# Two weight folds placed together, with one weight load moved forward and two weight loads cut into smaller pieces

## The chip, the cores and the metric

The kernel runs on one core of a Trainium2 chip. The core has five engines that run their own instruction streams: TensorE (PE in the profile, with its weight loads listed as PEld), VectorE (DVE), ScalarE (ACT), GpSimd (POOL) and SyncE (SP). Here SyncE issues all DMA transfers. The metric is the time of one execution on the device in microseconds; the median over the runs counts.

## The reference

One token sequence of 2048 rows and 512 columns in bfloat16 goes through a layer norm, then through a linear attention and, in parallel, a gated feed-forward part; both are added to the input.

```python
xn = _layernorm(x)
# attention, 32 heads of width 16
qkv = (xn @ wqkv)                       # 512 -> 3 * 512, by heads
pq, pk = q @ w_phi[h], k @ w_phi[h]     # 16 x 16 per head
phi = concat(softmax(p), softmax(-p))   # for q and for k
kv, z = phi_k^T v, sum over s of phi_k
o = (phi_q kv) / (phi_q z + 1e-6)
# feed-forward, width 1792
h = (xn @ w_gate) * (xn @ w_up)
out = x + o @ wo + h @ w_down
```

## The kernel before

The 2048 tokens are 16 tiles of 128 (n = 0 to 15), four tiles to a group (T = 0 to 3). The normalized tokens are kept transposed in xnT (features on the partitions). Tiles 0 to 3 are transposed on TensorE. For the others, `ln_block` leaves a list of chores: statistics on VectorE, the inverse deviation on GpSimd, the normalized tile `xn` on ScalarE and a DMA transpose into xnT issued by SyncE (L222). `chore(k)` runs the next k of them.

The feature weights are folded once: wq and wk are each multiplied by the block-diagonal of w_phi, so that W1q and W1k give pq and pk straight from xnT. `fold` does half of one of them: it needs `wT2`, which holds wq and wk transposed by a DMA from device memory (index 0 is wq, 1 is wk), and `bd`, the block-diagonal. It fills two PSUM banks with 16 small matmuls of 64 rows (two row halves side by side) and copies one bank on ScalarE and one on VectorE. `fold_both` calls it for both halves. The W1k fold stands between units 2 and 3; the W1q fold stands at tile 7 of the main loop, and the load of wq's transposed part is issued at L450, just before that loop.

A unit (T, f) of the feed-forward part is four matmuls for the gate block f, four for the up block f (each 128x512, over one group of tokens), a ScalarE copy of the gate and a VectorE product into hT. There are 14 blocks (FC) for each of 4 groups. `ffn(k)` issues the next k units. The units fill the time of TensorE between the projections: `vkproj(n)` computes v and the k features of tile n (eight matmuls), `features` makes exponentials on ScalarE, sums and reciprocals on VectorE and the product on GpSimd, `kv(n)` adds the tile to the attention state, and `qproj(n)` makes the q features. Later `attend` and `fin` finish each tile.

The order on every engine is written out by hand: the program's order is the order of each engine's stream. SyncE's stream begins with the loads at L84 to L102: x tiles 0 to 3 between pieces of wv, gate and up weights of blocks 0 to 3, w_phi, wk transposed (L96), gate and up blocks 4 to 8 (L97), x tiles 4 to 7 (L98), blocks 9 to 13 (L99), x tiles 8 to 15, w_down, wo. The transposes of xnT tiles 4 to 7 come behind them in the same queue.

Eight PSUM banks are there. Six of them rotate (`bank`, pool ps_s) for all projections, units and folds; the other two belong in turn to pv of tiles 0 and 1 (pool ps_v), to the attention state (ps_k) and to the attention output (ps_ab).

Of the kernel before, what the change touches and what calls it, by code (L numbers as in the profile page):

```python
# [16 lines left out]
def _bcast_ap(ap_in: bass.AP, new_ap):  # L17
    return bass.AP(tensor=ap_in.tensor, offset=ap_in.offset, ap=new_ap)
# [3 lines left out]
def kernel(  # L22
# [12 lines left out]
    nc = tc.nc  # L35
    P = 128
    S, D = A_x.shape[-2], A_x.shape[-1]
# [4 lines left out]
    DC = D // P  # L42
    FC = F // P
# [3 lines left out]
    TT = GT * P  # L47
# [16 lines left out]
    wv = wpool.tile([P, DC, D], BF16)  # L64
# [7 lines left out]
    wT2 = hpool.tile([P, 2, DC, D], BF16, name="wT2", tag="h")  # L72

    def dma_x(lo, hi):
        nc.sync.dma_start(out=xall[:, lo:hi, :], in_=x_view(lo, hi))  # L75

    def dma_cols(eng, w, src, lo, hi, at=0):
        eng.dma_start(out=w[:, :, lo - at:hi - at], in_=src[:, lo:hi].rearrange("(c p) f -> p c f", p=P))

    def dma_gu(lo, hi):  # L80
        dma_cols(nc.sync, wg, B_w_gate, lo * P, hi * P)
        dma_cols(nc.sync, wu, B_w_up, lo * P, hi * P)
# [3 lines left out]
    for lo in (0, 2):  # L86
        nc.sync.dma_start(out=wv[:, lo:lo + 2, :],  # L87
                          in_=A_wqkv[lo * P:(lo + 2) * P, 2 * D:3 * D].rearrange("(c p) f -> p c f", p=P))
# [4 lines left out]
    dma_cols(nc.sync, wu, B_w_up, 0, 2 * P)  # L93
    nc.sync.dma_start(out=wphi[:], in_=A_w_phi.rearrange("(c h) d f -> (h d) c f", c=DC))
    dma_gu(2, 4)
    nc.sync.dma_start(out=wT2[:, 1, :, :], in_=A_wqkv[:, D:2 * D], transpose=True)  # L96
    dma_gu(4, 9)  # L97
    dma_x(4, 8)  # L98
    dma_gu(9, FC)  # L99
    dma_x(8, NT)  # L100
    nc.sync.dma_start(out=wd[:], in_=B_w_down.rearrange("(c p) d -> p c d", p=P))
    nc.sync.dma_start(out=wo[:], in_=A_wo.rearrange("(c p) n -> p c n", p=P))  # L102
# [25 lines left out]
    W1q = wpool.tile([P, DC, D], BF16)  # L128
    W1k = wpool.tile([P, DC, D], BF16)
# [20 lines left out]
    def bank(name, dt=F32, n=TT):  # L150
        return ps_s.tile([P, n], dt, name=name, tag="s")
# [49 lines left out]
    def chore(k=1):  # L201
        for _ in range(min(k, len(chores))):
            chores.pop(0)()
# [40 lines left out]
        nc.vector.tensor_tensor(out=bd[:], in0=_bcast_ap(bo, [bo.ap[0], [0, DC], [E1, 8], [1, DH]]),  # L244
                                in1=_bcast_ap(wp, [wp.ap[0], [DH, DC], [0, 8], [1, DH]]), op=ALU.mult)

    def fold(qk, dst, j0):
        R = P // 2
        banks = [bank("pq").rearrange("p (j c x) -> p j c x", j=2, c=DC) for r in range(2)]
        for j in range(2):  # L250
            for c in range(DC):
                for r in range(2):
                    rows = slice(r * R, (r + 1) * R)
                    nc.tensor.matmul(banks[r][:, j, c, :], lhsT=wT2[rows, qk, c, (j0 + j) * P:(j0 + j + 1) * P],  # L254
                                     rhs=bd[rows, c, 4 * r:4 * r + 4, :].rearrange("p a b -> p (a b)"),
                                     start=True, stop=True)
        dv = dst[:, j0:j0 + 2, :].rearrange("p j (c r x) -> p r j c x", c=DC, r=2)
        nc.scalar.copy(out=dv[:, 0], in_=banks[0])
        nc.vector.tensor_copy(out=dv[:, 1], in_=banks[1])

    def fold_both(qk, dst):
        for j0 in (0, 2):
            fold(qk, dst, j0)

    def proj(ps, n, w, js=range(DC)):
        for j in js:
            nc.tensor.matmul(ps, lhsT=xnT[:, j, n * P:(n + 1) * P], rhs=w[:, j, :],  # L267
                             start=(j == 0), stop=(j == DC - 1))
# [21 lines left out]
    def qproj(n):  # L290
        phiq = features(n, W1q, "q")
        phiqTs[n] = qtpool.tile([P, NG, P], BF16, name="phiqT")
        nc.sync.dma_start(out=phiqTs[n][:], in_=phiq[:].rearrange("p g c -> p (g c)"), transpose=True)

    hTs = {}
    units = [(T, f) for T in range(NGRP) for f in range(FC)]

    def half(w, name, T, f, lo, hi):
        ps = bank(name)[:, 0:hi - lo]
        for c in range(DC):  # L300
            nc.tensor.matmul(ps, lhsT=w[:, c, f * P:(f + 1) * P], rhs=xnT[:, c, T * TT + lo:T * TT + hi],  # L301
                             start=(c == 0), stop=(c == DC - 1))
        return ps

    def gate_copy(ps, n):
        g_sb = gpool.tile([P, TT], BF16, name="g_sb")
        nc.scalar.copy(out=g_sb[:, 0:n], in_=ps)  # L307
        return g_sb

    def hidden(T, f, ps, g_sb, lo, hi):  # L310
        if T not in hTs:
            hTs[T] = hpool.tile([P, FC, TT], BF16, name="hT", tag="h")
        nc.vector.tensor_tensor(out=hTs[T][:, f, lo:hi], in0=ps, in1=g_sb[:, 0:hi - lo], op=ALU.mult)  # L313

    def unit(T, f, lo=0, hi=TT):
        pg = half(wg, "g", T, f, lo, hi)
        pu = half(wu, "u", T, f, lo, hi)
        hidden(T, f, pu, gate_copy(pg, hi - lo), lo, hi)

    def ffn(k):  # L320
        for _ in range(k):
            if units:
                unit(*units.pop(0))
# [31 lines left out]
    def vcopy(n, ps, eng=nc.scalar):  # L355
        dst, src = vts[n % NV][:, :, :, 0:DH], ps.rearrange("p (a b c) -> p a b c", a=8, b=4)
        if n >= GT:
            nc.scalar.copy(out=dst, in_=src)  # L358
        elif eng is nc.scalar:
            nc.scalar.activation(out=dst, in_=src, func=AF.Identity, scale=rst[:, n:n + 1])  # L360
        else:
            eng.tensor_scalar(out=dst, in0=src, scalar1=rst[:, n:n + 1], scalar2=None, op0=ALU.mult)

    with tc.tile_pool(name="ps_v", bufs=1, space=PSUM) as ps_v:
        pv = [ps_v.tile([P, D], F32, name=f"pv{n}") for n in range(2)]
# [32 lines left out]
        nc.gpsimd.tensor_tensor(out=r2[:], in0=rst[:], in1=rst[:], op=ALU.mult)  # L398
        nc.gpsimd.tensor_tensor(out=M4[:], in0=BO[:, 0:4, :], in1=BO[:, 4:8, :], op=ALU.add)

    with tc.tile_pool(name="ps_k", bufs=1, space=PSUM) as ps_k:
        kvps = [ps_k.tile([P, 4, 4, E1], F32, name=f"kv{b}") for b in range(2)]
        phiks = {}

        def kproj(n, pf=None):
            phiks[n] = features(n, W1k, "k", pf)

        def vkproj(n, apart=False):
            pv, pk = bank("pv"), bank("k")
            for js in (range(DC),) if apart else [(j,) for j in range(DC)]:  # L410
                proj(pv, n, wv, js)
                proj(pk, n, W1k, js)
            vcopy(n, pv)
            kproj(n, pk)

        def kv(n):
            vt, phik = vts[n % NV], phiks[n]
            for gr in range(NG):
                nc.tensor.matmul(kvps[gr // 4][:, gr % 4, :, :].rearrange("p a b -> p (a b)"),  # L419
                                 lhsT=phik[:, gr, :], rhs=vt[:, gr, :, :].rearrange("p a b -> p (a b)"),  # L420
                                 start=(n == 0 and gr % 4 == 0), stop=(n == NT - 1 and gr % 4 == 3))

        for f in range(2):
            unit(0, f, 2 * P, TT)
        del units[0:2]
        ffn(1)
        fold_both(1, W1k)
        ffn(1)
        ln_block(4)
        ffn(1)  # L430
        chore(2)
        kproj(0)
        ffn(1)
        chore(2)
        ffn(1)
        chore()
        kproj(1)
        ffn(1)
        chore()
        ffn(1)  # L440
        kproj(2)
        chore()
        ffn(1)
        kv(0)
        chore()
        kproj(3)
        chore()
        ffn(1)
        kv(1)
        nc.sync.dma_start(out=wT2[:, 0, :, :], in_=A_wqkv[:, 0:D], transpose=True)  # L450
        for n in range(GT, NT):
            if n in (4, 8):
                ln_block(n + 4)
            if n == 7:
                fold_both(0, W1q)
            vkproj(n, apart=n == 7)
            chore(1 if n % GT < 2 else 0)
            ffn(1)
            kv(n - 2)
            if n == 6:  # L460
                ffn(1)
            chore((1, 2, 2, 2)[n % GT])
            if n >= 8 and n % 2 == 0:
                qproj((n - 8) // 2)
            if n != 6:
                ffn(1)
        ffn(1)
        kv(NT - 2)
        ffn(1)
        kv(NT - 1)  # L470
        for b in range(2):
            nc.vector.tensor_tensor(out=KV[:, 4 * b:4 * b + 4, :, :], in0=kvps[b][:],
                                    in1=_bcast_ap(M4[:], [M4[:].ap[0], [0, 4], [E1, 4], [1, E1]]), op=ALU.mult)
        qproj(4)
        ffn(1)
# [65 lines left out]
```

## Time and profile before

| what | value |
|---|---|
| median of 3 runs | 221.17 us (221.03 to 221.37) |
| profiled execution | 221.16 us |
| its span | 219.5 us |
| TensorE clock granted | 1.00 |
| VectorE busy | 140.0 us |
| ScalarE busy | 88.4 us |
| GpSimd busy | 72.8 us |
| read from device memory | 8.67 MB |

Busy times are sums over the span; an engine can be busy much of it without setting the end. A row of the costliest groups gives line, engine, operation, what it writes and reads, the count, the busy time and the mean of one. Times "to landing" of a DMA count from the start of its issue on SyncE until its completion is signalled.

### The profile page before, as it was taken

To read this page: it belongs to the slowest core of one execution; us is meant where nothing else is said; L and a number is where in the kernel's file an instruction comes from. 1 tells how busy PE (TensorE), PEld (TensorE's weight loads), DVE (VectorE), ACT (ScalarE), POOL (GpSimd) and SP (SyncE) were. 2 spreads that over 40 slices of the span, in tenths; PEclk is the share of its full clock that TensorE was granted. 3 is DMA by queue.
4 is the path that set the end of the run, shared out by engine and by line. 5 is a ranking of instruction groups with operands and counts; after the bars stand their busy time and mean duration, and the time that the engine had idled before them with its cause. 6 is when DMAs were issued, how large, how long until landed. Compare 5 with 4: busy or idle time off the path is not lost.

```text
span 219.5 us, 3521 instructions
## 1 busy us (share of the span) xinstructions
PE 215.4 (98%) x1307; PEld 104.4 (48%) x1307; DVE 140.0 (64%) x240; ACT 88.4 (40%) x164; POOL 72.8 (33%) x64
## 2 busy tenths in 40 slices
PE   8999999999999999999999999999999999999994
PEld 3564445445444444444544444444444444454443
DVE  5757976887598757667499773196655645454321
ACT  4635496449664775465435212141231322100000
POOL 3600655363348463635145333033023033000000
PEclk9999999999999999999999999999999999999999
DMA  5999994303202241202047345114431431412501
GB/s 156 260 302 390 371 249 99 49 0 51 48 0 48 51 73 24 48 3 48 1 27 121 72 106 118 43 24 96 96 75 24 96 75 25 96 48 72 74 25 48
DMA packets 47249, 19.91 MB, mean 91 GB/s; under 512 B 37504, under 2 KB 46976, under 8 KB 47104
## 3 DMA queue, kind: packets, MB, share of 16 engines
q1 hardware_dynamic: 47232, 19.69, 38.7%
q8 instruction: 10, 0.16, 0.3%
q14 instruction: 7, 0.06, 0.1%
HBM read 8.67 MB, written 2.10 MB: 49 GB/s over the span
## 4 chain that ended last, share of the span: by engine, by line
PE 96%; DMA 2%; SPq 1%; issue 0%; DVE 0%
PE g L301 22%; PE fin L331 22%; PE u L301 22%; PE fin L334 6%; PE k L267 6%; PE q L267 6%; PE pv L267 6%; DMA wv<-in_A_wqkv_dram 2%; PE kv L419 2%; PE ab L483 2%; SPq L75 1%; PE pq L254 1%; SPq L87 0%; DVE o_sb L342 0%; PE tp L235 0%
## 5 line engine op out<-in xcount | busy, mean ns | idle before, releaser
L301 PE MATMUL u<-xnT,wu 128*128 128x512 bf16 (+1 forms) x232 | 57.8, 372 | 0.0
L301 PE MATMUL g<-xnT,wg 128*128 128x512 bf16 (+1 forms) x232 | 57.7, 372 | 0.0
L307 ACT CAST g_sb<-g 128x512 bf16<-128x512 f32 (+1 forms) x58 | 33.4, 576 | 48.6 <-PE g L301 48.4
L313 DVE TENSOR_TENSOR hT<-u,g_sb 128x512 bf16<-128x512 f32 (+1 forms) x58 | 37.1, 648 | 24.6 <-PE u L301 15.5
L286 POOL TENSOR_TENSOR phiq<-e,rs 128x1024 bf16<-128x1024 f32 x16 | 30.9, 1932 | 62.9 <-DVE rs L284 54.1
L282 DVE TENSOR_REDUCE sums<-e 128x64 f32<-128x1024 f32 x32 | 38.9, 1216 | 20.2 <-ACT e L278 20.2
L331 PE MATMUL fin<-wd,hT 128*128 128x512 bf16 (+2 forms) x238 | 51.1, 366 | 0.0
L286 POOL TENSOR_TENSOR phik<-e,rs 128x1024 bf16<-128x1024 f32 x16 | 30.9, 1931 | 43.9 <-DVE rs L284 30.3
L301 PEld LDWEIGHTS <-wu 128*128 128x128 bf16 x232 | 22.7, 98 | 25.6
L331 PEld LDWEIGHTS <-hT 128*128 128x128 bf16 x238 | 22.4, 98 | 24.8
L301 PEld LDWEIGHTS <-wg 128*128 128x128 bf16 x232 | 22.0, 98 | 23.6
L267 PEld LDWEIGHTS <-xnT 128*128 128x128 bf16 x192 | 17.3, 98 | 18.8 <-ACT xnT L238 1.3
L267 PE MATMUL pv<-wv,xnT 128*128 128x512 bf16 x64 | 22.1, 381 | 0.4 <-DMA wv<-in_A_wqkv_dram 0.2
L267 PE MATMUL k<-W1k,xnT 128*128 128x512 bf16 x64 | 21.8, 379 | 0.0
L342 DVE TENSOR_TENSOR o_sb<-fin,xall 128x512 bf16<-128x512 f32 (+2 forms) x13 | 8.5, 651 | 20.5 <-PE fin L334 20.5
L284 DVE RECIPROCAL rs<-sums 128x64 f32<-128x64 f32 x32 | 17.7, 553 | 3.1
L334 PE MATMUL fin<-wo,oT 128*128 128x512 bf16 (+2 forms) x68 | 16.6, 366 | 0.0
L267 PE MATMUL q<-W1q,xnT 128*128 128x512 bf16 x64 | 16.4, 378 | 0.0
L276 ACT ACTIVATE e<-q 128x512 f32<-128x512 f32 x12 | 7.2, 597 | 22.2 <-PE q L267 22.2
L358 ACT CAST vt<-pv 128x512 bf16<-128x512 f32 x12 | 7.1, 588 | 16.4 <-PE pv L267 16.4
L493 DVE TENSOR_TENSOR otok<-ab,rden 128x512 bf16<-128x512 f32 x16 | 11.1, 691 | 0.6
L157 DVE BATCH_NORM_STATS2 stats<-xall 128x6 f32<-128x512 bf16 x16 | 10.7, 670 | 1.0 <-DMA xall<-in_A_x_dram 1.0
(60 smaller groups left out, 126.3 us busy)
## 6 DMA issues: line engine op xcount, KB each, us to landing
out_dram<-o_sb SPq DMA_DIRECT2D x15, 128.0 KB, 1.9
wd<-in_B_w_down_dram SPq DMA_DIRECT2D x1, 1792.0 KB, 15.4
wg<-in_B_w_gate_dram SPq DMA_DIRECT2D x2, 640.0 KB, 6.9
wu<-in_B_w_up_dram SPq DMA_DIRECT2D x2, 640.0 KB, 8.0
xall<-in_A_x_dram SPq DMA_DIRECT2D x1, 1024.0 KB, 11.7
xall<-in_A_x_dram SPq DMA_DIRECT2D x4, 128.0 KB, 2.5
wv<-in_A_wqkv_dram SPq DMA_DIRECT2D x2, 256.0 KB, 3.6
wg<-in_B_w_gate_dram SPq DMA_DIRECT2D x2, 256.0 KB, 4.8
```

Of the source, the lines that this page charges most:

```text
L157: nc.vector.bn_stats(out=stats[:], in_=xall[:, n, :])
L267: nc.tensor.matmul(ps, lhsT=xnT[:, j, n * P:(n + 1) * P], rhs=w[:, j, :], start=(j == 0), stop=(j == DC - 1))
L282: nc.vector.tensor_reduce(out=sums[:], in_=ev, axis=AX.X, op=ALU.add)
L284: nc.vector.reciprocal(out=rs[:].rearrange("p a b -> p (a b)"), in_=sums[:])
L286: nc.gpsimd.tensor_tensor(out=phi[:].rearrange("p g (x f) -> p (g x) f", f=DH), in0=ev, in1=rs[:].to_broadcast((P, 2 * H, DH)), op=ALU.mult)
L301: nc.tensor.matmul(ps, lhsT=w[:, c, f * P:(f + 1) * P], rhs=xnT[:, c, T * TT + lo:T * TT + hi], start=(c == 0), stop=(c == DC - 1))
L307: nc.scalar.copy(out=g_sb[:, 0:n], in_=ps)
L313: nc.vector.tensor_tensor(out=hTs[T][:, f, lo:hi], in0=ps, in1=g_sb[:, 0:hi - lo], op=ALU.mult)
L331: nc.tensor.matmul(ps, lhsT=hTs[T][:, f, t4 * P:(t4 + 1) * P], rhs=wd[:, f, lo:lo + w], start=(f == 0), stop=False)
L334: nc.tensor.matmul(ps, lhsT=oTs[n][:, c, :], rhs=wo[:, c, lo:lo + w], start=False, stop=(c == DC - 1))
L342: nc.vector.tensor_tensor(out=o_sb[:], in0=ps, in1=xres, op=ALU.add)
L493: nc.vector.tensor_tensor(out=o_tok[:].rearrange("p (b h d) -> p b h d", b=2, d=DH), in0=abv[:, :, :, 0:DH], in1=rden[:].to_broadcast((P, ...
```

## The change

Four things change. The load of wq's transposed part moves from L450 to right behind wk's. Gate and up weights of blocks 4 to 13 come in loads of blocks 4 and 5, 6 to 9 and 10 to 13, with x tiles 4 to 7 behind the first of them. The second halves of units 0 and 1, then units 2 and 3, then all four half folds follow each other; the first half of W1q uses the two banks that held pv of tiles 0 and 1, so the folds stand now within that pool's scope. In the main loop the W1q fold, the special place of one unit at tile 6, and the form of `vkproj` that does v's four matmuls before k's at tile 7 are gone.

```diff
-    nc.sync.dma_start(out=wT2[:, 1, :, :], in_=A_wqkv[:, D:2 * D], transpose=True)
-    dma_gu(4, 9)
+    for qk in (1, 0):
+        nc.sync.dma_start(out=wT2[:, qk, :, :], in_=A_wqkv[:, qk * D:(qk + 1) * D], transpose=True)
+    dma_gu(4, 6)
     dma_x(4, 8)
-    dma_gu(9, FC)
+    dma_gu(6, 10)
+    dma_gu(10, FC)
     dma_x(8, NT)
...
-    def fold(qk, dst, j0):
+    def fold(qk, dst, j0, pq):
         R = P // 2
-        banks = [bank("pq").rearrange("p (j c x) -> p j c x", j=2, c=DC) for r in range(2)]
+        banks = [ps.rearrange("p (j c x) -> p j c x", j=2, c=DC) for ps in pq]
...
-    def fold_both(qk, dst):
-        for j0 in (0, 2):
-            fold(qk, dst, j0)
...
         nc.gpsimd.tensor_tensor(out=M4[:], in0=BO[:, 0:4, :], in1=BO[:, 4:8, :], op=ALU.add)
 
+        for f in range(2):
+            unit(0, f, 2 * P, TT)
+        del units[0:2]
+        ffn(2)
+        for qk, dst in ((1, W1k), (0, W1q)):
+            for j0 in (0, 2):
+                own = qk == 0 and j0 == 0
+                fold(qk, dst, j0, [ps[:] if own else bank("pq") for ps in pv])
+
...
-        def vkproj(n, apart=False):
-            pv, pk = bank("pv"), bank("k")
-            for js in (range(DC),) if apart else [(j,) for j in range(DC)]:
-                proj(pv, n, wv, js)
-                proj(pk, n, W1k, js)
-            vcopy(n, pv)
+        def vkproj(n):
+            ps, pk = bank("pv"), bank("k")
+            for j in range(DC):
+                proj(ps, n, wv, (j,))
+                proj(pk, n, W1k, (j,))
+            vcopy(n, ps)
             kproj(n, pk)
...
-        for f in range(2):
-            unit(0, f, 2 * P, TT)
-        del units[0:2]
-        ffn(1)
-        fold_both(1, W1k)
-        ffn(1)
         ln_block(4)
         ffn(1)
...
-        nc.sync.dma_start(out=wT2[:, 0, :, :], in_=A_wqkv[:, 0:D], transpose=True)
         for n in range(GT, NT):
             if n in (4, 8):
                 ln_block(n + 4)
-            if n == 7:
-                fold_both(0, W1q)
-            vkproj(n, apart=n == 7)
+            vkproj(n)
             chore(1 if n % GT < 2 else 0)
             ffn(1)
             kv(n - 2)
-            if n == 6:
-                ffn(1)
             chore((1, 2, 2, 2)[n % GT])
             if n >= 8 and n % 2 == 0:
                 qproj((n - 8) // 2)
-            if n != 6:
-                ffn(1)
+            ffn(1)
```

## The prediction

> **What bounds the kernel now.** I read the page's first and fourth parts first, then TensorE's own timeline, then SyncE's, and last the load of the DMA engines by stretches.
>
> ```profile
> PE 215.4 (98%) x1307; PEld 104.4 (48%) x1307; DVE 140.0 (64%) x240; ACT 88.4 (40%) x164; POOL 72.8 (33%) x64
> PE 96%; DMA 2%; SPq 1%; issue 0%; DVE 0%
> ```
>
> TensorE is busy 98% of the span, and the chain that ended last is TensorE's for 96%. In the list of waits of that engine only two stand, 0.8 us at the start and 0.2 us before the first projections. So from about 7 us on the time is the sum of TensorE's instructions in their order. An edit can gain only by taking work off TensorE, and it loses whatever stall it puts there.
>
> What the two folds cost on TensorE is read from the chain in order of time (start us, us, what):
>
> ```profile
> 15.38 0.57 PE pq L254 x32
> 15.96 0.97 PE g L301 x4
> 16.93 0.86 PE u L301 x4
> ...
> 50.14 0.57 PE pq L254 x32
> 50.72 0.97 PE pv L267 x4
> 51.69 0.86 PE k L267 x4
> ```
>
> A fold of both j halves is 32 small matmuls in 0.57 us, and the four full matmuls right behind it take 0.97 where others of their size take 0.86: each return from 64-row to 128-row tiles costs 0.11 us.
>
> The loads all go through SyncE's queue (start us, us of issue):
>
> ```profile
> 7.28 3.53 SPq L96 DMA_TRANSPOSE wT<-in_A_wqkv_dram  x1
> 10.86 0.58 SPq L78 DMA_DIRECT2D wg<-in_B_w_gate_dram  x1
> ...
> 16.10 8.28 SPq L102 DMA_DIRECT2D wo<-in_A_wo_dram  x1
> 28.69 7.08 SPq L222 DMA_TRANSPOSE xnT<-xn  x4
> 35.82 2.16 SPq L450 DMA_TRANSPOSE wT<-in_A_wqkv_dram  x1
> ```
>
> The load of wq's part stands behind all others at 35.82, after the four transposes of token tiles 4 to 7. How full the DMA engines are comes from the stretches (columns: stretch, its us, then busy us and count for PE, PEld, DVE, ACT, POOL, then TensorE's clock, DMA share, GB/s):
>
> ```profile
> 11.00:12.00 1.00, 1.00 (x7) 0.52 (x6) 0.38 (x1) 0.09 (x1) 0.00 (x0) 1.00 1.28 290
> 12.00:13.00 1.00, 1.00 (x12) 0.90 (x10) 0.98 (x2) 0.37 (x1) 0.00 (x0) 1.00 0.88 117
> 14.00:16.00 2.00, 2.00 (x40) 1.05 (x39) 0.70 (x2) 0.83 (x2) 0.00 (x0) 1.00 1.06 385
> 24.00:30.00 6.00, 6.00 (x30) 2.69 (x28) 5.21 (x10) 3.89 (x7) 5.20 (x6) 1.00 1.08 351
> 30.00:33.00 3.00, 3.00 (x23) 1.47 (x22) 2.32 (x3) 3.00 (x6) 0.85 (x2) 1.00 1.00 157
> ```
>
> Until about 30 us the DMA engines have no free time. And this is where the queue touches TensorE: the transposes of tiles 4 and 5, in the issues of the stretches around 28.7 and 31.0 us:
>
> ```profile
> xnT<-xn SPq DMA_TRANSPOSE x1, 4.3
> ...
> xnT<-xn SPq DMA_TRANSPOSE x1, 2.4
> ```
>
> Tile 4's transpose is issued at 28.69 and lands 4.3 us later, at 33.0; tile 5's needs 2.4 us. The difference is the backlog: wo's load, issued at 16.10 and 16.4 us on its way, lands at 32.5, just ahead of it. TensorE's timeline starts the first projection of tile 4 at 33.68. The slack is 0.7 us.
>
> The page "DMA: Bandwidth & Descriptors" of the Trainium skill (section Queues, rings and completion order) says that each DMA engine takes SyncE's descriptors in ring order; the trace agrees, 4.3 us against 2.4.
>
> **The change part by part.**
>
> *TensorE's work.* The same instructions in another order. The q fold's 0.57 us leaves 50.14 and goes to about 17.1 (units 2 and 3 first, then k's fold, then q's). One of the two returns to full tiles goes: -0.11 us. Interleaving pv and k for tile 7, as for the other tiles, changes no count: in the chain a group of eight such matmuls takes 1.72 us in either form, less the 0.11 after the fold. So TensorE reaches tile 4's projection at 33.68 + 0.57 = 34.25, and without a stall the end moves by -0.11.
>
> *PSUM banks and evictions around the folds.* Unit 3's up matmuls end at 15.38 + 1.73 = 17.11 in the new order. Banks rotate by six; q's first half has the two pv banks, so the only tight pair is q's second half, which takes unit 3's banks. Their reader on VectorE (0.69 us, begun 0.11 us after unit 2's up matmuls in the old trace) is done at 17.91, while three of four halves (48 matmuls of 18 ns) occupy TensorE to 17.97. I price this at 0, bounds 0 to 0.2. Unit 4's gate, at 18.25, needs the first ScalarE copy (0.59 us, from about 17.5): covered. Four copies each on ScalarE (1.07 us a pair) and VectorE (1.28 a pair) run to 19.6 and 20.5, so unit 4's product starts near 20.5 instead of 19.62. Behind it stand tile 4's and 5's statistics and tile 0's k sums; this delays tile 4's normalized tile and the issue of its transpose from 28.69 to some 29.5. With 2.4 us to land that would be 31.9, still ahead of 34.25. So 0 on the path. At 50.9 to 52 four copies go from ScalarE and VectorE; TensorE did not wait there, so nothing is gained.
>
> *The load of wq's part, moved in front.* It passes, on SyncE, ten loads in the new cut (six of gate and up weights, two of x, wd, wo) and four token transposes. The DMA engines are full, so everything behind it shifts by its own time. k's part, the same 512 KB, ran at 290 GB/s in the stretch 11 to 12: 0.524 MB / 290 GB/s = 1.81 us. Lower bound: the stretch 12 to 13, just behind k's transpose, moved 117 GB/s where 385 would go, 0.70 us lost; if the second transpose fills that hole, 1.1. Upper bound: SyncE spent 3.53 us on issuing k's and issues nothing else meanwhile, 3.5. I take 1.81, as the stretch is the same operation under the same load.
>
> The same page (section Latency and other measured facts) gives 261 GB/s for a DMA transpose with a non-contiguous middle dimension; by that it would be 2.0 us and the end 0.2 later. The row decides for 290.
>
> *Gate and up weights in pieces of 2, 4 and 4 column blocks instead of 5 and 5.* Same 2560 KB, 1.28 KB rows cut to 0.5 and 1 KB. Before: 2.62 MB at 377 GB/s (385 in 14 to 16, 369 in 18 to 21) = 6.95 us. After: 0.52 MB at the 301 GB/s of 6 to 9 us, when pieces of 0.5 KB ran, = 1.74, and 2.10 MB at the 351 GB/s of 24 to 30, where wd's and wo's 1 KB rows run, = 5.97. Together 7.71: +0.76 us for all that follows. Bounds 0 (the 301 is mixed with tiny packets of wphi, and rows may cost nothing) to 0.8.
>
> *Sum.* The queue ahead of tile 4's transpose ends 1.81 + 0.76 = 2.57 us later, so the transpose lands at 33.0 + 2.57 = 35.57. TensorE is there at 34.25 and waits 1.32 us; no other matmul can pass. Behind the waiting projection stand, in order, unit 11, kv of tile 2 and all the rest; nothing later has idle time on TensorE to give it back. Total 1.32 - 0.11 = +1.2 us. Against the profiled execution's 221.16 us (span 219.5), which is the median of 221.17 to 0.01: 222.4 us, or 0.5% slower. In general the end moves by the queue's shift less 1.36, and by -0.11 at the least.
>
> **The rivals.**
>
> *The queue is shifted by less than tile 4's slack of 1.25 us* (the other sign: not slower). Place: the landing of tile 4's transpose. Price: none, only the merged fold's -0.11 us remains, 221.05 us; it decides below a shift of 1.25. For it: the 0.70 us hole at 12 to 13 us, and pieces that may cost less than I take: 1.1 + 0 is enough. Against it: DMA share at or above 1 in all stretches but that one, and wo's landing half a microsecond ahead of the transpose's.
>
> *The weights become late first.* The up weights for unit 6 lie now in the load of blocks 6 to 9. Of the old load of blocks 9 to 13 the up part landed at 13.28 + 10.0 = 23.3. Now a wq part (1.81), 0.5 MB in small pieces (1.74) and 1 MB in 1 KB rows (1.05 MB / 351 = 2.99) take the place of 6.95 us: 22.9. Unit 6's up matmuls come at 22.80 + 0.57 = 23.37: in time by 0.5. If the issue time of 3.53 holds, it is 24.6 and TensorE waits 1.2 us there, and the rest of the late transpose's delay falls at tile 4: the landing shifts by 3.53 + 0.76 = 4.29, the end by 4.29 - 1.36 = 2.9, 224.1 us. For it: k's own issue. Against it: that issue came while other loads filled the queue, and the late one took 2.16.
>
> *The merged folds gain more than the one return.* At most all that the q fold costs, 0.57 + 0.11 = 0.68 us: 220.5. For it: nothing but that the small matmuls overlap in two row groups; against it, both folds took the same 0.57 in the old trace, wherever they stood. The change does what it says on SyncE and TensorE, where both orders are written out by hand, so that it does nothing is no case.
>
> **How the numbers follow.** What can be told from no change here is 0.2%, 0.44 us. The forecast (tile 4 waits, shift of 1.8 to 3.3 us) gets 0.54; the shift that stays in the slack, or over it by less than 0.44 + 0.11 us, gets 0.28; the large shift with late weights 0.10; the gain beyond one return 0.08. So faster 0.08, same 0.28, slower 0.64. The forecast's own range is 221.6 to 223.1. The range for 8 in 10 reaches down to the rival without a stall with some spread of single runs (220.9) and up to a shift of 3.9 us (223.7).
>
> **What would show it.** In the changed profile: two fold groups as one run of 64 small matmuls of 1.14 us near 17.1, with one 0.97 behind them; the late fold at 50 gone; a wait of TensorE, or of its weight load, on a DMA at the first projection of tile 4, at 34.3 to 35.6 us; tile 4's transpose landing some 6 us after its issue; wo landing near 35 instead of 32.5. I am wrong if TensorE shows no wait between 30 and 40 us, if wo lands before 33.8, if the wait stands already at units 4 to 6, or if the time is under 221 with the folds shorter than 1.1 us.

## The result and the profile after

The changed kernel takes 223.73 us, the median of 6 runs (223.07 to 226.15), against 221.12 us before (220.98 to 221.37). The ratio of all runs is 1.0145, interval 1.011 to 1.018. Two of the six runs, 225.98 and 226.15 us, had a mean granted clock of 0.992 and the others 0.999 or 1.000; the median of these four is 223.58 us. Forecast were 222.4 us and a range of 220.9 to 223.7: the direction and the place of the wait hold, the size is too small by half. The profiled execution took 223.65 us, its span 221.9 (before 221.16 and 219.5): +2.5 us.

The first and fourth parts of the page of the changed kernel:

```profile
PE 215.4 (97%) x1307; PEld 104.3 (47%) x1307; DVE 140.0 (63%) x240; ACT 88.5 (40%) x164; POOL 72.9 (33%) x64
PE 90%; DMA 3%; DVE 3%; ACT 1%; issue 1%; POOL 1%; DVEq 0%
```

TensorE's busy time is the same to 0.1 us, as it must be when only the order changes. The 2.5 us are idle time of TensorE, and the chain that ended last now runs through a DMA. Who waited for whom, for TensorE and for its weight loads (us in total, times, longest):

```profile
PE pv L265 <- DMA xnT<-xn: 1.8, 1, 1.8
...
PE g L299 <- ACT W1q L260: 0.7, 1, 0.7
...
PEld L299 <- DMA wg<-in_B_w_gate_dram: 0.8, 1, 0.8
```

Two waits have come, and TensorE's timeline shows where (start us, us; in brackets the idle time before):

```profile
16.75 0.64 PE L256 MATMUL pq<-bd,wT 64*128 64x64 bf16 x32
17.22 0.40 PE L256 MATMUL pv<-bd,wT 64*128 64x64 bf16 x16
17.45 0.60 PE L256 MATMUL pq<-bd,wT 64*128 64x64 bf16 x16
18.74 1.04 PE L299 MATMUL g<-xnT,wg 128*128 128x512 bf16 x4 [0.69 <-ACT W1q L260]
...
34.55 0.42 PE L426 MATMUL kv<-vt,phik 128*128 128x68 bf16 x8
36.77 0.39 PE L265 MATMUL pv<-wv,xnT 128*128 128x512 bf16 x1 [1.81 <-DMA xnT<-xn]
```

The second is the forecast one: the first projection of tile 4 starts at 36.77 instead of 33.68, 1.81 us after TensorE was ready. The first, 0.69 us at unit 4, stands against a ScalarE copy in one list and against the gate weights' DMA in the other; the experiments decide for the DMA. It costs nothing here, since tile 4 could not have started earlier anyway: the end moves by 36.77 - 33.68 less the 0.66 us that the late q fold took between its neighbours before, 2.43 us, and the span by 2.4.

SyncE's queue (start us, us of issue), then the landing of wo's load and of tile 4's transpose:

```profile
7.25 5.65 SPq L97 DMA_TRANSPOSE wT<-in_A_wqkv_dram  x2
12.94 0.58 SPq L78 DMA_DIRECT2D wg<-in_B_w_gate_dram  x1
...
14.67 2.64 SPq L78 DMA_DIRECT2D wg<-in_B_w_gate_dram  x1
17.36 0.51 SPq L78 DMA_DIRECT2D wu<-in_B_w_up_dram  x1
```

```profile
wo<-in_A_wo_dram SPq DMA_DIRECT2D x1, 512.0 KB, 14.9
...
xnT<-xn SPq DMA_TRANSPOSE x1, 6.9
```

wo is issued at 21.36 and lands at 36.2 (before 32.5); tile 4's transpose is issued at 29.81 and lands at 36.7 (before 33.0). Both are 3.7 us later. The issue of the gate weights of blocks 6 to 9 took 2.64 us where its neighbours take 0.5. Three stretches of the changed kernel (columns as in the prediction; the last three are TensorE's clock, DMA share, GB/s):

```profile
12.00:13.00 1.00, 1.00 (x12) 0.90 (x10) 1.00 (x3) 0.41 (x2) 0.00 (x0) 1.00 0.74 147
...
17.80:19.00 1.20, 0.51 (x17) 0.28 (x13) 1.20 (x3) 1.20 (x3) 0.00 (x0) 1.00 0.73 150
19.00:22.00 3.00, 3.00 (x16) 1.35 (x15) 2.25 (x4) 1.28 (x3) 0.00 (x0) 1.00 1.07 368
```

The reader is to see two holes: one between the two transposes at 12 to 13 us, and one at 17.8 to 19.0, behind the long issue, where the DMA engines moved 150 GB/s.

### The profile page after: what moved, and what is told of

It reads as the page before. It is cut to its first block, busy times and chain, and to the rows that moved or that the text cites. A ratio compares the mean times of both kernels' runs of the same rounds, so it can differ in the third digit from the quotient of the medians.

```text
span 221.9 us, 3521 instructions
## 1 busy us (share of the span) xinstructions
PE 215.4 (97%) x1307; PEld 104.3 (47%) x1307; DVE 140.0 (63%) x240; ACT 88.5 (40%) x164; POOL 72.9 (33%) x64
## 4 chain that ended last, share of the span: by engine, by line
PE 90%; DMA 3%; DVE 3%; ACT 1%; issue 1%; POOL 1%; DVEq 0%
PE fin L329 22%; PE g L299 20%; PE u L299 19%; PE pv L265 6%; PE fin L332 6%; PE q L265 6%; PE k L265 5%; DMA xnT<-xn 3%; PE ab L478 2%; PE kv L426 2%; PE warm L348 1%; DVE stats L159 1%; DVE hT L311 1%; DVE sums L280 1%; PE tp L237 0%
## 5 line engine op out<-in xcount | busy, mean ns | idle before, releaser
L284 POOL TENSOR_TENSOR phik<-e,rs 128x1024 bf16<-128x1024 f32 x16 | 30.9, 1932 | 46.4 <-DVE rs L282 33.5
L329 PEld LDWEIGHTS <-hT 128*128 128x128 bf16 x238 | 22.4, 98 | 24.8
L265 PEld LDWEIGHTS <-xnT 128*128 128x128 bf16 x192 | 17.3, 97 | 20.7 <-DMA xnT<-xn 1.9
L265 PE MATMUL k<-W1k,xnT 128*128 128x512 bf16 x64 | 22.3, 379 | 0.0
```

The costliest lines, as they stand in the source:

```text
L284: nc.gpsimd.tensor_tensor(out=phi[:].rearrange("p g (x f) -> p (g x) f", f=DH), in0=ev, in1=rs[:].to_broadcast((P, 2 * H, DH)), op=ALU.mult)
L329: nc.tensor.matmul(ps, lhsT=hTs[T][:, f, t4 * P:(t4 + 1) * P], rhs=wd[:, f, lo:lo + w], start=(f == 0), stop=False)
```

## The experiments

The theory: what is queued ahead of tile 4's transpose is pushed back, and TensorE waits there. Rivals: the four half folds in a row cost by their eight copies and banks; the smaller pieces cost by SyncE's issues; tile 4 is late because its normalized tile is late. All times are medians; "lands" is tile 4's transpose in the profiled run.

| kernel | us | ratio to before (interval) | lands | waits of TensorE after 8 us |
|---|---|---|---|---|
| before | 221.1 to 221.2 | | 33.0 | none |
| changed | 223.73 | 1.0145 (1.011 to 1.018) | 36.7 | 0.69 unit 4, 1.81 tile 4 |
| e1 wq's load early, alone | 226.12 | 1.0222 (1.0178 to 1.0266) | 36.1 | 2.3 and 0.7 unit 4 |
| e2 pieces alone | 221.35 | 1.0015 (1.0003 to 1.0027) | 33.6 | none |
| e3 changed, old pieces | 223.68 | 1.0114 (1.0097 to 1.0131) | 36.3 | 1.8 and 0.7 unit 4 |
| e4 changed, wd and wo late | 221.49 | 1.0018 (1.0008 to 1.0028) | 32.0 | 0.3 unit 4 |
| e5 as e4, wq behind blocks 4 and 5 | 222.57 | 1.0083 (1.005 to 1.0115) | 35.9 | 1.7 q fold |
| e6 folds alone | 221.04 | 0.9992 (0.9983 to 1.0001) | 33.8 | none listed |
| e7 changed, wo late | 222.01 | 1.0035 (1.0023 to 1.0047) | 35.1 | 0.6 unit 4 |
| e8 as e4, more warm-up matmuls | 221.96 | 1.0038 (1.0021 to 1.0055) | 31.9 | none |
| e9 as e5, folds behind unit 4 | 221.36 | 1.001 (1.0001 to 1.0019) | 33.8 | 0.3 unit 6 |

### e1, wq's load early, alone

```diff
     nc.sync.dma_start(out=wT2[:, 1, :, :], in_=A_wqkv[:, D:2 * D], transpose=True)
+    nc.sync.dma_start(out=wT2[:, 0, :, :], in_=A_wqkv[:, 0:D], transpose=True)
...
-        nc.sync.dma_start(out=wT2[:, 0, :, :], in_=A_wqkv[:, 0:D], transpose=True)
```

> The kernel before with one edit: the load of wq's transposed part stands right behind wk's; folds and weight pieces stay as they were. Queue theory: all loads behind it shift by 1.8 us (524 KB at 290 GB/s) to 2.5 us (with a stretch in which the DMA engines starve, as in the changed kernel at 17.8 to 19.0 us), tile 4's transpose lands at 34.8 to 35.5 instead of 33.0, TensorE is there at 33.68 and waits 1.1 to 1.8 us: 222.3 to 223.0 us. Theory that the order of the folds makes the loss: no change, 221.1 us.

Measured 226.12 us, far over both. TensorE's waits in e1, and the stretch behind them:

```profile
PE g L302 <- DMA wg<-in_B_w_gate_dram: 2.3, 1, 2.3
...
PE u L302 <- DMA wu<-in_B_w_up_dram: 0.7, 1, 0.7
```

```profile
22.00:27.00 5.00, 5.00 (x18) 2.04 (x17) 2.81 (x6) 1.74 (x3) 0.00 (x0) 0.72 1.05 396
```

With the old large pieces the weights of unit 4 come with 640 KB each and land at 19.9 and 21.6 us, so TensorE stands at unit 4 and not at tile 4; and after 3.0 us of waits the mean granted clock of the next five microseconds was 0.72, an estimated 1.4 us more. The queue itself answers the question: wo, issued at 19.87, takes 15.7 us and lands at 35.6 instead of 32.5. The load moved alone shifts the queue by 3.1 us, not by 1.8.

### e2, the pieces alone

```diff
-    dma_gu(4, 9)
+    dma_gu(4, 6)
     dma_x(4, 8)
-    dma_gu(9, FC)
+    dma_gu(6, 10)
+    dma_gu(10, FC)
```

> The kernel before with one edit: gate and up weights of blocks 4 to 13 in pieces of 2, 4 and 4 blocks with x tiles 4 to 7 behind the first. Queue theory: a shift of 0.76 us at most, against a slack of 0.68 us at tile 4: 221.1 to 221.3 us. Theory that the pieces themselves, by SyncE's longer issues, make the loss: a long issue and a starved stretch here too, 222 us or more.

Measured 221.35 us, a hair above the 221.1 to 221.3, and no wait of TensorE after its first projections. wo lands at 18.86 + 14.3 = 33.2 and tile 4's transpose at 33.6, both 0.6 us later than before, just inside the slack. So the pieces cost the queue 0.6 us and are not the loss; e1's 3.1 and these 0.6 make the changed kernel's 3.7.

### e3, the changed kernel with the old pieces

```diff
-    dma_gu(4, 6)
+    dma_gu(4, 9)
     dma_x(4, 8)
-    dma_gu(6, 10)
-    dma_gu(10, FC)
+    dma_gu(9, FC)
```

> The changed kernel with the old pieces (blocks 4 to 8, x tiles 4 to 7, blocks 9 to 13). Queue theory: tile 4's transpose lands 0.7 us earlier than in the changed kernel (36.0 instead of 36.7), so 222.8 to 223.1 us, but unit 4's weights come with a larger piece and TensorE waits for them 1 us or more (hidden in the later wait). If the pieces were the cause of the starved stretch: no starved stretch, tile 4's transpose at 35 or earlier, 222.2 us or less.

Measured 223.68 us (222.31 to 225.45; the profiled execution is the slowest of the five). The stretch 17.8 to 19.0 moved 401 GB/s and is not starved. But e7 below, with the small pieces, moved 370 there, and e4 334, so the pieces alone do not make that stretch; what else does is open. wo lands at 35.8, only 0.4 us earlier than in the changed kernel, and the weights of unit 4 now hold TensorE for 2.5 us in the profile. Tile 4's transpose is issued only at 33.5 behind that wait and lands at 36.3, when TensorE has not yet come to it. So the pieces decide where TensorE waits, at unit 4 or at tile 4; the time is the same.

### e4, wd and wo behind the transposes of tiles 4 to 7

```diff
     dma_x(8, NT)
-    nc.sync.dma_start(out=wd[:], in_=B_w_down.rearrange("(c p) d -> p c d", p=P))
-    nc.sync.dma_start(out=wo[:], in_=A_wo.rearrange("(c p) n -> p c n", p=P))
...
+        nc.sync.dma_start(out=wd[:], in_=B_w_down.rearrange("(c p) d -> p c d", p=P))
+        nc.sync.dma_start(out=wo[:], in_=A_wo.rearrange("(c p) n -> p c n", p=P))
         for n in range(GT, NT):
```

> The changed kernel with one edit: the loads of wd and wo are issued behind the transposes of tiles 4 to 7, so that nothing is queued ahead of these. Queue theory: tile 4's transpose lands 2.4 to 3.2 us after its issue near 29.8, no wait of TensorE there; what is left is the wait of 0.7 us at unit 4, less 0.11: 221.7 us. Theory that tile 4 is late because its statistics and its normalized tile are late (folds on VectorE and ScalarE): the wait stays, 223 us or more.

Measured 221.49 us; tile 4's transpose lands 2.4 us after its issue at 29.52, and of TensorE's waits after the start one is left:

```profile
PE g L297 <- DMA wg<-in_B_w_gate_dram: 0.3, 1, 0.3
```

Taking 2.25 MB of loads out of the way gives back all but 0.4 us of the loss. That a late normalized tile makes the loss is out: its transpose was issued nearly as late here (29.52 against 29.81).

### e7, wo alone behind them

```diff
-    nc.sync.dma_start(out=wo[:], in_=A_wo.rearrange("(c p) n -> p c n", p=P))
...
+        nc.sync.dma_start(out=wo[:], in_=A_wo.rearrange("(c p) n -> p c n", p=P))
         for n in range(GT, NT):
```

> The changed kernel with wo's load alone (512 KB) moved behind the transposes of tiles 4 to 7; wd's stays ahead. Queue theory: tile 4's transpose lands earlier by wo's own time, 524 KB at 351 GB/s = 1.5 us, at 35.2, against an arrival of TensorE at 34.96 that has unit 4's wait in it: a wait of 0 to 0.4 us there, 221.8 to 222.2 us. If it were not the bytes queued ahead but something else that makes tile 4 late, less than a third of the 1.5 us comes back: 223.2 us or more.

Measured 222.01 us. The transpose lands at 35.1, 1.6 us earlier for 512 KB less ahead of it; TensorE, held 0.6 us at unit 4, is ready for tile 4 at 35.03 and starts it at 35.12. The delay goes with the bytes in the queue.

### e6, the folds alone

```diff
-                    nc.tensor.matmul(banks[r][:, j, c, :], lhsT=wT2[rows, qk, c, (j0 + j) * P:(j0 + j + 1) * P],
+                    nc.tensor.matmul(banks[r][:, j, c, :], lhsT=wT2[rows, 1, c, (j0 + j) * P:(j0 + j + 1) * P],
...
-    for qk in (1, 0):
-        nc.sync.dma_start(out=wT2[:, qk, :, :], in_=A_wqkv[:, qk * D:(qk + 1) * D], transpose=True)
+    nc.sync.dma_start(out=wT2[:, 1, :, :], in_=A_wqkv[:, D:2 * D], transpose=True)
```

The weight pieces are the old ones here. wq's transposed part is not loaded; W1q is folded from wk's, so the q of this kernel is not the reference's.

> The changed kernel's order of folds and units without its loads: wq's transposed part is not loaded, W1q is folded from wk's part instead (so the attention's q is not the reference's), and the weight pieces are the old ones. Queue theory: no wait of TensorE between 8 and 40 us, and the time is 0.11 us below the kernel before: 221.03 us. Theory that the folds in a row cost by their copies and banks: a wait of 0.3 to 0.7 us at unit 4, 221.4 us or more.

Measured 221.04 us, ratio 0.9992 (0.9983 to 1.0001), and no wait in TensorE's list after its first projections: the copies and banks do not make unit 4's wait of the changed kernel, which is the weights' DMA. The time is the expected one, but its interval, 0 to -0.4 us, cannot tell the forecast gain of 0.11 us from none. The traces can: from unit 2's first matmul to the end of the last one it is 203.10 us in e6 (13.67 to 216.77) and 203.11 before (13.49 to 216.60). Nothing is gained. TensorE's timeline of e6, its chain there in order of time, and VectorE's product of unit 3:

```profile
16.26 1.03 PE L297 MATMUL u<-xnT,wu 128*128 128x512 bf16 x4
17.22 0.64 PE L254 MATMUL pq<-bd,wT 64*128 64x64 bf16 x32
17.70 0.40 PE L254 MATMUL pv<-bd,wT 64*128 64x64 bf16 x16
17.93 0.60 PE L254 MATMUL pq<-bd,wT 64*128 64x64 bf16 x16
18.46 1.04 PE L297 MATMUL g<-xnT,wg 128*128 128x512 bf16 x4
```

```profile
17.86 0.23 PE pv L254 x16
18.09 0.03 PE pq L254
18.12 0.02 issue
18.14 0.39 PE pq L254 x15
```

```profile
17.39 0.69 DVE L309 TENSOR_TENSOR hT<-u,g_sb 128x512 bf16<-128x512 f32 x1 [1.04 <-PE u L297]
```

From the first small matmul to the gate behind, the run of 64 takes 18.46 - 17.22 = 1.24 us. Before, the two runs of 32 took 0.58 (15.31 to 15.89) and 0.57 (50.08 to 50.65), 1.15 together. The extra time is one break: the first of the last 16 starts at 17.93, the second only at 18.14, where small matmuls otherwise start at most 0.04 us apart. The last half fold writes into unit 3's banks, and that second matmul waits for a semaphore of VectorE, whose product of unit 3 ends at 18.08, 0.05 us before it. The same break of 0.21 us, with the same 0.05 us behind the product's end, stands in the traces of the changed kernel, e3, e4, e7, e8 and e9. It is missing from the list of waits because the modelled end of the matmul before covers it. Without the break the run of 64 would take an estimated 1.04 us, 0.11 less than the two runs, as forecast; and the change into small matmuls, 0.10 us (16.26 to 17.22 is 0.96 for four matmuls of 0.86), is paid once instead of twice. The merged folds gain 0.2 us and the bank takes 0.2 us back.

### e5 and e9, a version without the waits

e5 is e4 with wq's load behind the first pieces; e9 also moves the folds behind unit 4.

```diff
-    for qk in (1, 0):
-        nc.sync.dma_start(out=wT2[:, qk, :, :], in_=A_wqkv[:, qk * D:(qk + 1) * D], transpose=True)
+    nc.sync.dma_start(out=wT2[:, 1, :, :], in_=A_wqkv[:, D:2 * D], transpose=True)
     dma_gu(4, 6)
+    nc.sync.dma_start(out=wT2[:, 0, :, :], in_=A_wqkv[:, 0:D], transpose=True)
```

> The kernel of e4 (wd and wo behind the transposes of tiles 4 to 7) with wq's transposed load moved behind the weights of blocks 4 and 5. Queue theory: these weights land near 15 us instead of 18.4 (e2 had them at 14.1 and 15.1 without the second transpose), so TensorE's wait at unit 4 goes and the time is 221.05 us, or up to 0.5 more if the q fold at 17.4 us now waits for its load (1.8 us of transfer behind 15 us and the time to completion). Theory that the folds' eight copies hold unit 4's PSUM banks: a wait of 0.3 to 0.7 us stays at unit 4, released by a ScalarE or VectorE copy, 221.4 us or more.

Measured 222.57 us (222.05 to 224.88). Unit 4 waits no more, but the q fold does, by more than I allowed for; the profiled execution is the slowest of the six:

```profile
PE pv L254 <- DMA wT<-in_A_wqkv_dram: 1.7, 1, 1.7
```

The load was issued at 12.64 and landed at 19.7. In e9:

```diff
-        ffn(2)
+        ffn(3)
         for qk, dst in ((1, W1k), (0, W1q)):
...
         kproj(0)
         ffn(1)
-        chore(2)
-        ffn(1)
-        chore()
+        chore(3)
         kproj(1)
```

> The kernel of e5 with the four half folds behind unit 4 instead of unit 3, and one unit less between tile 0's and tile 1's k projections, so that the later units stand as before. The q fold comes at 19.1 us, where e5's load of wq's part had landed at 19.7 with one late engine and at 18.2 on the others. Queue theory: a wait of 0 to 0.6 us for that load, none at unit 4 and none at tile 4: 221.05 to 221.7 us, the lower end beating the kernel before by the 0.11 us of one return to full tiles. Theory that early folds cost by the copies and banks: a wait at unit 5 released by a copy, 221.5 us or more.

Measured 221.36 us, ratio 1.001 (1.0001 to 1.0019): inside the expected span, but not below the kernel before. One wait is left, at unit 6, the place that the prediction's second rival had worked out:

```profile
PE u L297 <- DMA wu<-in_B_w_up_dram: 0.3, 1, 0.3
```

With the wait for unit 3's bank in them the merged folds gain 0.01 us (e6), so there is nothing here to beat the old kernel with. An order of the half folds that leaves that bank alone was not run; by e6's rows it would be worth an estimated 0.2 us.

### e8, more instructions in TensorE's stream

```diff
-    warm_up(7)
+    warm_up(5)
+    warm_up(24, 16)
     warm_up(1, P)
```

> The kernel of e4 with 24 narrow warm-up matmuls (16 columns) in place of two wide ones at the start: 22 matmuls and as many weight loads more in TensorE's stream. If the 16 KB instruction packet that runs on one DMA engine (15.9 us in e4, 14.6 in the changed kernel) brings TensorE's own instructions, it comes 2 to 4 us earlier, and the lag of one DMA engine behind the others moves with it, so that unit 4's weights lag at another place and the wait at unit 4 (0.3 us) changes. If it has nothing to do with TensorE's stream: packet and wait stay where they were, 221.3 to 221.6 us.

Measured 221.96 us (221.31 to 222.91), slower than e4; the profiled execution is the fastest of the seven. The instruction packet came at 14.1 us instead of 15.9, and the later ones 0.3 to 5.5 us earlier than e4's, most of them by over 3; 44 instructions are 3.7 us of TensorE's stream at 12 a microsecond. That it brings TensorE's instructions fits. At 14.1 us it hits wq's transpose, and this is the DMA view of e8's stretch 13 to 16 us in 40 slices (busy tenths, GB/s, and the queue of instruction packets):

```profile
DMA  8965999393109999990000000000000000000199
GB/s 154 147 116 123 246 263 96 72 65 31 10 17 96 171 488 276 263 147 0 0 0 0 0 0 0 0 0 7 7 7 10 10 7 10 10 10 10 41 287 283
...
q8 instruction: 1, 0.02, 2.0%
```

From 14.35 to 15.0 us nothing is moved, and until 15.8 us no more than 10 GB/s. The transpose lands at 17.3 instead of 15.5, but then unit 4's gate weights have no late engine and land at 18.2 on all sixteen: the wait at unit 4 is gone in this profile.

## Why the prediction was wrong, point by point

*What bounds the kernel*: right. TensorE's busy time did not change, and the loss is idle time of TensorE at the place named, the first projection of tile 4. e4 and e7 show that the bytes queued ahead of its transpose make it.

*"I take 1.81, as the stretch is the same operation under the same load"*: this is the step that failed. wq's load costs the queue 3.1 us (e1: wo at 35.6 against 32.5). That is inside the term's own bounds of 1.1 to 3.5. The transfer rate was right: wq's part ran at 289 GB/s (e1, 13.6 to 14.6 us). Two things were left out. First, the hole that I saw behind k's transpose and set only as a possible gain is there after each transpose: in e1 12 to 13 us moved 149 GB/s and 14.5 to 16.5 moved 239, where 290 and 385 go, so 0.49 + 0.76 us are lost against 0.70 before: +0.55. Second, the last of the sixteen DMA engines falls further behind the others. The completion signals of wd's load in the traces, one from each engine:

```
            first   last    last - first
before      29.30   31.01   1.71
e2          29.59   31.74   2.15
e1          31.62   34.09   2.47
changed     32.66   34.90   2.24
```

In e1 the first engine is 2.32 us late, where 1.81 + 0.55 makes 2.36, and the last one 3.08. It is a single engine that trails: fifteen had signalled by 32.39, the sixteenth came 1.70 us later. A transfer has landed when the last engine is done. My rows of GB/s are means over sixteen engines and cannot show that. In the changed kernel the starved stretch takes (385 - 150) / 385 of 1.2 us = 0.73 more from the first engine, which so stands at 2.32 + 0.29 (e2) + 0.73 = 3.34 (measured 3.36), and the lag is a little smaller. The shift of 3.1 is measured by e1 alone; this splitting of it is an estimate from rows, and no run that keeps wd and wo in the queue takes the hole or the lag away.

*The pieces, 0.76 us*: 0.6 measured alone (e2); right within its bounds.

*The merged folds, -0.11*: right for the return to full tiles, and the 0.10 us of one change into small matmuls was left out; a bank wait eats both, -0.01 in all (e6).

*Banks and evictions, 0, bounds 0 to 0.2*: wrong by all of the bound; 0.20 us (e6). The prediction names the pair, q's second half in unit 3's banks behind a product on VectorE. What failed is the pace: 18 ns a matmul is the mean of a run of 32 with both changes of tile size in it. Three halves take 0.71 us (17.22 to 17.93), not 0.86, and TensorE is there before VectorE is done. In the changed kernel this adds nothing, as unit 4's weights are later still. The page's "W1q" as releaser of unit 4 is a wrong name: the wait shrinks or goes with the weights' landing (e4, e5, e8), not with the copies.

*The sum, shift less 1.36*: the form holds. With 3.7 us of shift instead of 2.57 it gives 2.37; the profiled execution took 2.49 more. The two errors at the folds do not show in it: the early folds end before a wait that would be there anyway.

*Weights late first*: I worked it out for unit 6 (in time) and did not work out unit 4, whose gate weights landed at 18.7 against a start at 18.05. By its own signs the prediction has this against it: a wait already at units 4 to 6. In the changed kernel that wait is hidden behind tile 4's. Its price shows where nothing follows it: 0.3 us in e4's profile, 0.6 in e7's.

*Not slower, within the slack*: out; e2 alone stays there. *The range* ended at a shift of 3.9 us with 223.7, a hair under the median of 223.73.

## What to carry to other kernels

Before a load is moved forward in a full queue, look for the last small transfer behind it that the bounding engine needs, and its slack; here a 128 KB transpose with 0.7 us of slack stood behind 2.25 MB that nobody needed before 119 us, and moving those behind it gave back 2.2 of the 2.6 us (e4). Price a load in such a queue by the landing of what stands behind it, on the slowest DMA engine, not by its bytes over a rate. A large first piece holds up what is needed next: unit 4 waited 2.5 us with the old pieces (e3) and 0.7 with the small ones. A mean per instruction over a run is not the pace inside it: look for the changes of form at its ends before a bank's reuse is priced with it.

## What the runs showed of the hardware

- A pause of TensorE can lower its clock for some microseconds after it. In the traces of e1, e3 and e5 the granted clock falls to 0.50 for 3.4 us each (21.4 to 24.8, 21.5 to 25.0 and 20.4 to 23.8 us), after waits of 2.3 and 0.7, of 1.8 and 0.7, and of 1.7 us; in the changed kernel's profile a wait of 1.81 us left it at 1.00. "TensorE: Matmul & The Clock Gate" in the Trainium skill (section Part 1: The HAM clock gate) gives an idle window of about 3.4 us; here 1.7 us was enough once, and 1.81 once not. What decides is not shown, and the changed kernel's two runs at a mean clock of 0.992 (e1's and e5's profiled runs have that mean) were not profiled.
- One 16 KB instruction packet comes at 14 to 18 us among the loads. SyncE's issue that fell on it was long, 2.64 us from 14.67 with the packet at 14.63 to 16.94 (changed kernel), 2.12 from 15.44 with it at 15.29 to 17.15 (e7); but in e2 an issue of 3.09 us began 2.1 us before the packet, so that the packet makes it long is not shown. Where the packet fell into wq's transpose, the DMA engines together moved about 10 GB/s or less for 1.5 us (e8) and for 1.1 us (e9, 17.0 to 18.1). That the packet alone makes the lag of the last engine is not shown: e1's took 0.97 us, and the last signal of unit 4's gate weights came 1.85 us behind the fifteenth.
